# The first chunk of the projections, started on two token tiles instead of four

## The chip, the cores and the metric

One core of one Trainium2 chip runs the whole kernel in one launch. The metric is the device time of the launch in microseconds (us), given as the median of several runs. PE is the matrix engine, PEld its weight loads, DVE the vector engine, ACT the scalar engine, POOL is GpSimd, and SP is the engine that issues most DMAs.

## The reference: what is computed

A pre-norm transformer block on 2048 tokens of width 640, in float32: attention with 32 heads of width 20, then a gated feed-forward part of width 1728.

```
x = A_x
h = x + _A_ref(_layernorm(x, axis=-1), A_wqkv, A_wo)
h2 = h + _B_ref(_layernorm(h, axis=-1), B_w_gate, B_w_up, B_w_down)
```

The change lies in the very first step: the layernorm of the first 512 tokens and their products with `A_wqkv`, which give queries, keys and values.

## The kernel before

**Precision.** PE multiplies in a rounded form of float32. An operand is therefore split into a high part (a rounded copy, written by ACT) and a low part (the operand less its high part, written by DVE or POOL). A product is then three products: high by high, low by high, high by low. `w_hi` and `w_lo` hold the two parts of `wqkv`; `z_hi` and `z_lo` hold those of the normalised and transposed tokens.

**Tiles.** Tokens come in 4 chunks of 512, each of 4 tiles of 128. `wqkv` is cut into 15 blocks of 128 columns: blocks 0 to 9 hold keys (even) and queries (odd), blocks 10 to 14 hold the values. A DMA (`load_w(i)`, L541 to L549) brings two blocks at a time into one of four buffers named `raw`; a fifth load waits until a buffer is free.

**The order of work.** The schedule is written by hand: every engine executes its instructions in the order in which the program issues them. The start of the projections (L814 to L838) goes so. SP issues the loads of the four token tiles (`load_x(0)`), then four weight loads. POOL fills 32 rows twice in `k_stk` with ones (`fill_ones`, L153). PE runs three plain float32 products whose result is not used (`warm`, L820), on the token tile that is loaded last. `norm(0)` computes mean and variance of all four tiles on DVE (L137, L138), then one reciprocal square root for all four by 14 small DVE instructions (L111), then normalises the four tiles (L574). ACT writes the high parts of weight blocks 0 and 1 (L826). `flip_tokens(t)` (L624) transposes a tile on PE in five pieces (L628) into a two-bank PSUM buffer; ACT writes its `z_hi` and DVE its `z_lo` (L101, L102). After the third tile, `first_blocks` (L720) multiplies blocks 0 and 1 with the 256 tokens of the first two tiles, high by high alone. The low parts of weight blocks 0 and 1 follow on DVE (L833).

**The first slots.** The rest of the chunk is a list of 18 slots. Slot 0 issues `split_w` for blocks 2 to 5 (high parts on ACT, low parts on DVE), then the remaining `first_blocks` products for blocks 0 and 1, then `keep` for both, which takes a finished block out of PSUM, splits it, and sends it to DRAM from POOL's queue. Slot 1 frees the PSUM banks of `flip_tokens` and hands them to a pool of six single banks. Slots 2 to 9 are blocks 2 to 9 by `query_key`, then 8 slots of values. From block 6 on `split_w` puts the low parts on POOL.

**`rounds`** (L658) issues the 15 products of a block in halves: one on the upper 64 rows of the array now, the other half on the lower 64 rows 20 steps later (`LAG`), so that two halves of different products run side by side. Blocks rotate over three PSUM banks.

**The jobs in between.** In the gaps of this stream a planner places the search for score maxima that the later softmax needs (`max_four`: four products on PE, two ACT passes, four more products and two DVE reductions at L250). The planner keeps a modelled clock for each engine (`takes`). A job is placed when its keys and queries have been loaded back from DRAM, and a load may be issued from a slot that `stored_at` names. What is left of these jobs at the end runs in a closing loop; then attention begins.

Of the kernel before, what the change touches and what calls it, by code (L numbers as in the profile page):

```python
# [9 lines left out]
F32 = mybir.dt.float32  # L10
# [7 lines left out]
P = 128  # L18
S = 2048
D = 640  # L20
# [33 lines left out]
def tile_block(ctx: ExitStack, tc: tile.TileContext, x, wqkv, wo, wg, wu, wd, out):  # L54
# [27 lines left out]
    ps_ctx = ExitStack()  # L82
    flip_ctx = ExitStack()
    psum_two, psum_wide = (
        c.enter_context(tc.tile_pool(name=name, bufs=n, space=bass.MemoryType.PSUM))
        for c, name, n in ((ps_ctx, "psum_o", 2), (flip_ctx, "psum_w", 3))
    )
# [314 lines left out]
    with tc.tile_pool(name="pa", bufs=2) as pa:  # L402
# [7 lines left out]

        def load_x(c):
            for t in range(c * TPC, (c + 1) * TPC):
                xs[t] = x_tile()[:, :D]
                nc.sync.dma_start(xs[t], x[t * P : (t + 1) * P, :])
# [228 lines left out]
        LAG = 20  # L643
        given = [0, 0, 0]

# [49 lines left out]

        firsts = []

# [11 lines left out]

        def first_blocks(*hns):  # L710

            if not firsts:
                firsts.extend(ps_one() for _ in range(2))
            z_hi, z_lo = zs[0]
            for h, n in hns:
                cols = slice(h * CH // 2, (h + 1) * CH // 2)
                a, w = ((z_hi, w_hi), (z_lo, w_hi), (z_hi, w_lo))[n]
                for m, ps in enumerate(firsts):
                    for k in range(ND):
                        nc.tensor.matmul(  # L720
                            ps[:, cols], w[:, k, m * P : (m + 1) * P], a[:, k, cols],
                            start=(h == n == k == 0), stop=(h == 1 and n == 2 and k == ND - 1),
                        )

        def keep(c, m, ps):
# [87 lines left out]

        load_x(0)  # L814
        fill_ones(k_stk[0])
        for i in range(4):
            load_w(i)
        warm = ps_one()
        for _ in range(3):
            nc.tensor.matmul(warm, ident, xs[TPC - 1][:, :CH], start=True, stop=True)  # L820
        for _, _, f in norm(0):
            f()
        zs[0] = z_tiles(0)
        first_raw = raws.pop(0), raws.pop(1)
        for m, raw in enumerate(first_raw):
            nc.scalar.activation(w_hi[:, :, m * P : (m + 1) * P], raw, AF.Copy)  # L826
        for t in range(TPC):
            flip_tokens(t)
            if t == TPC - 2:
                first_blocks((0, 0))  # L830
        for m, raw in enumerate(first_raw):
            cs = slice(m * P, (m + 1) * P)
            nc.vector.tensor_tensor(  # L833
                out=w_lo[:, :, cs], in0=raw, in1=w_hi[:, :, cs].bitcast(F32), op=ALU.subtract
            )
# [4 lines left out]
        first = [("block", 0), ("none",)] + [("block", m) for m in range(2, 2 * ND)]  # L840
        some_keys = [("block", 2 * i) for i in range(ND)]
# [3 lines left out]
        for c in range(NC):  # L845
            lns = []
            work = (some_keys + some_queries if c else first) + parts
            if c == NC - 1:
# [3 lines left out]
                es.insert(1, z_tiles(NC)[0][:, :2])  # L852
            for j, (kind, *which) in enumerate(work):
                slot[0] = 18 * c + j
                while flips and not j:
                    flips.pop(0)()
                if c == 0 and j < 9:
                    for i in range(split_at[j], split_at[j + 1]):
                        split_w(i + 2)
# [18 lines left out]
                if which:  # L878
                    if (c, j) == (0, 0):
                        first_blocks((0, 1), (1, 0), (1, 1), (0, 2), (1, 2))  # L880
                        for m, ps in enumerate(firsts):
# [3 lines left out]
                else:  # L885
                    flip_ctx.close()
                    psum = ps_ctx.enter_context(
                        tc.tile_pool(name="psum", bufs=1, space=bass.MemoryType.PSUM)
                    )
                    turn, jobs, three = [0], [0], [0]  # L890

# [4 lines left out]
                    def ps_max():  # L896
                        n = turn[0] % 5
                        turn[0] += 1
                        if n > 2:
                            return psum_two.tile([P, CH], F32, name="ps_max", tag="ps_two")  # L900
                        three[0] += 1
                        return psum.tile([P, CH], F32, name="ps_max", tag=f"ps_max{three[0] % 3}")

# [51 lines left out]
    def ps_max():  # L955
        place[0] += 1
        return psum.tile([P, CH], F32, name="ps_max", tag=f"ps_max{place[0] % 3}")

# [1072 lines left out]
```

## Time and profile before

| | us |
|---|---|
| median of 3 runs | 2005.8 |
| the 3 runs | 2005.49, 2005.8, 2006.61 |
| the profiled execution, its own time | 2004.65 |
| span of its trace | 2002.9 |
| PE busy in the span | 1981.1 (99%) |
| DVE busy | 1604.4 (80%) |
| ACT busy | 1430.4 (71%) |
| POOL busy | 786.2 (39%) |

The span runs from the first to the last instruction of the trace; the execution's own time is 1.75 us longer. In a timeline row the first number is the start in us from the span's start, the second the length, then engine, line, operation, out<-in, shapes and a count when several like instructions were merged; the bracket at the end gives the idle time before and what ended it. In a row of windows each engine has its busy time with the number of instructions in brackets, followed by the clock granted to PE, the busy share of the DMA engines and GB/s. An instruction of PE or DVE shows a length that includes its way through the pipeline, so that the next one starts before its end; the distance between starts is the cost of one in a row of many.

### The profile page before, as it was taken

How to read it: one execution, taken by the hardware profiler on the slowest of the kernel's cores; microseconds unless marked ns; L12 is line 12 of the kernel's file. 1: busy time of each engine (PE TensorE's matmuls, PEld its weight loads, DVE VectorE, ACT ScalarE, POOL GpSimd, SP SyncE). 2: the span in 40 equal slices, each digit the busy share in tenths (PEclk: the TensorE clock that was granted, in tenths of full speed). 3: DMA queues.
4: the chain of work that ended last, by engine and by line, in shares of the span. 5: the costliest groups of instructions: out<-in, count | busy, mean ns of one | idle time of the engine just before them, and what ended most of it. 6: DMA issues, size and time to landing. Idle time of an engine off the chain costs nothing.

```text
span 2002.9 us, 41974 instructions
## 1 busy us (share of the span) xinstructions
PE 1981.1 (99%) x14792; PEld 1260.4 (63%) x14792; DVE 1604.4 (80%) x2873; ACT 1430.4 (71%) x2828; POOL 786.2 (39%) x1152
## 2 busy tenths in 40 slices
PE   8999999999999999999999999999999999999998
PEld 6999996444444444444444444455688888888887
DVE  5687778999999999999999999975478666677667
ACT  4677778999999999999999999977633221212221
POOL 6564423243252343334342111011255544844465
PEclk9999999999999999999999999999999999999999
DMA  7787563442533544435345222221268645974542
GB/s 239 258 258 258 176 208 90 129 121 97 161 104 114 150 135 130 130 111 157 120 134 161 79 73 60 77 67 59 65 207 291 235 159 180 358 243 166 199 147 93
DMA packets 197066, 310.50 MB, mean 155 GB/s; under 512 B 51368, under 2 KB 85480, under 8 KB 195832
## 3 DMA queue, kind: packets, MB, share of 16 engines
q1 hardware_dynamic: 190264, 284.21, 43.9%
q0 software_dynamic: 6496, 23.60, 3.9%
q8 instruction: 118, 1.93, 0.4%
q14 instruction: 92, 0.75, 0.1%
q10 hardware_dynamic: 96, 0.00, 0.0%
HBM read 208.11 MB, written 99.19 MB: 153 GB/s over the span
## 4 chain that ended last, share of the span: by engine, by line
PE 90%; DVE 1%; POOL 1%; ACT 1%; DMA 1%; issue 0%; SPq 0%; DVEq 0%; POOLq 0%; ACTq 0%
PE acc L1307 25%; PE ps_a L1494 15%; PE ps_one L1297 12%; PE ps_max L289 9%; PE ps_b L1588 8%; PE ps_max L261 7%; PE ps_one L667 7%; PE ps_max L228 3%; PE ps_max L1028 2%; PE ps_b L1028 1%; DMA t_d<-kept 0%; POOL h L1626 0%; DVE tmp L1709 0%; PE ps_max L1063 0%; POOL yp L102 0%
## 5 line engine op out<-in xcount | busy, mean ns | idle before, releaser
L1303 ACT ACTIVATE probs<-ps_one 128x512 f32<-128x512 f32 x2048 | 1049.2, 615 | 43.0 <-PE ps_one L1297 33.9
L267 DVE TENSOR_REDUCE found<-ps_max 128x1 f32<-128x512 f32 x980 | 630.4, 685 | 81.1 <-PE ps_max L261 63.7
L1297 PE MATMUL ps_one<-q_stk,k_stk 62*128 62x512 f32 x2048 | 571.9, 427 | 0.2 <-ACT probs L1303 0.2
L1307 PE MATMUL acc<-probs,v_stk 128*32 128x512 f32 x4096 | 546.6, 605 | 0.0
L289 PEld LDWEIGHTS ps_max<-k_stk,q_stk 60*128 60x128 f32 x984 | 181.8, 185 | 407.1 <-DVE found L267 402.7
L261 PE MATMUL ps_max<-k_stk,q_stk 60*128 60x512 f32 x980 | 392.9, 422 | 0.0
L298 DVE TENSOR_REDUCE found<-ps_max 128x2 f32<-128x512 f32 x492 | 335.1, 681 | 0.0
L289 PE MATMUL ps_max<-k_stk,q_stk 60*128 60x256 f32 x984 | 324.1, 329 | 0.0
L1297 PEld LDWEIGHTS ps_one<-q_stk,k_stk 62*128 62x128 f32 x2048 | 301.7, 184 | 20.0 <-ACT probs L1303 16.2
L1709 DVE TENSOR_TENSOR tmp<-ps_a,tmp 128x512 f32<-128x512 f32 x208 | 141.1, 689 | 119.7 <-PE ps_a L1494 94.0
L250 DVE TENSOR_REDUCE mx<-ps_max 128x2 f32<-128x512 f32 x288 | 180.7, 685 | 69.1 <-PE ps_max L228 61.8
L261 PEld LDWEIGHTS ps_max<-k_stk,q_stk 60*128 60x128 f32 x980 | 181.0, 185 | 52.1 <-DVE found L298 21.6
L1588 PE MATMUL ps_b<-halves,yp 128*128 128x320 f32 x1032 | 179.3, 308 | 2.0 <-POOL yp L102 1.2
L240 ACT ACTIVATE ps_max<-ps_max 128x512 f32<-128x512 f32 x288 | 151.4, 584 | 40.9 <-PE ps_max L228 38.9
L1588 PEld LDWEIGHTS ps_b<-halves,yp 128*128 128x128 f32 x1032 | 165.1, 188 | 18.7 <-POOL yp L102 1.5
L1494 PE MATMUL ps_a<-t,units 128*128 128x512 f32 x624 | 162.6, 396 | 0.0
L1307 PEld LDWEIGHTS acc<-probs,v_stk 128*32 128x32 f32 x4096 | 81.0, 108 | 128.5 <-issue 118.3
L102 POOL TENSOR_TENSOR yp<-y,yp 128x256 fp32r<-128x256 f32 x96 | 60.2, 627 | 188.2 <-ACT yp L101 188.2
L1494 PE MATMUL ps_a<-z,units 128*128 128x512 f32 x516 | 133.9, 394 | 0.0
L1494 PEld LDWEIGHTS ps_a<-t,units 128*128 128x128 f32 x624 | 112.5, 188 | 18.6
L1342 POOL TENSOR_TENSOR o<-o,rb 128x512 f32<-128x512 f32 x31 | 39.8, 1285 | 212.1 <-DMA q_stk<-q_d 80.0
L319 POOL CAST both<-neg 128x16 fp32r<-128x16 f32 x22 | 4.3, 197 | 299.0 <-DVE neg L309 243.5
(220 smaller groups left out, 3077.3 us busy)
## 6 DMA issues: line engine op xcount, KB each, us to landing
units<-w_d SPq DMA_DIRECT2D x186, 256.0 KB
w_d<-stage SPq DMA_DIRECT2D x106, 256.0 KB
halves<-j_d SPq DMA_DIRECT2D x70, 320.0 KB
j_d<-stage SPq DMA_DIRECT2D x42, 320.0 KB
k_stk<-k_d SPq DMA_DIRECT2D x64, 160.0 KB
q_stk<-q_d SPq DMA_DIRECT2D x64, 160.0 KB
raw<-k_d SPq DMA_DIRECT2D x62, 160.0 KB
raw<-q_d SPq DMA_DIRECT2D x54, 160.0 KB
```

The costliest lines, as they stand in the source:

```text
L240: nc.scalar.activation(ps, ps, AF.Relu)
L250: nc.vector.tensor_reduce(mx[:, b, :, t, kc], ps.rearrange("p (j n) -> p j n", j=2), axis=AX.X, op=ALU.max,)
L261: nc.tensor.matmul(ps, queries[u][rows, pair, t * P : (t + 1) * P], keys[u // NC][rows, pair, kc * CH : (kc + 1) * CH], start=True, stop=True,
L267: nc.vector.tensor_reduce(found_of(u)[:, b, pair, t, kc : kc + 1], ps, axis=AX.X, op=ALU.max)
L289: nc.tensor.matmul(ps[:, b * CH // 2 : (b + 1) * CH // 2], queries[u][rows, pair, t * P : (t + 1) * P], keys[u // NC][rows, pair, first : ...
L298: nc.vector.tensor_reduce(found_of(u)[:, :, pair, t, column], ps.rearrange("p (b n) -> p b n", b=2), axis=AX.X, op=ALU.max,)
L1297: nc.tensor.matmul(ps, keys[u // NC][rows, p, kt * P : (kt + 1) * P], queries[u][rows, p, :], start=True, stop=True,)
L1303: nc.scalar.activation(probs[p][:, b, :], ps, AF.Exp, scale=scale)
L1307: nc.tensor.matmul(acc[32 * j : 32 * j + 32, :], values[u // NC][:, kt, j * VW : j * VW + 32], probs[j // 2][:, j % 2, :], start=(kt == 0) ...
L1494: nc.tensor.matmul(ps.rearrange("p (t n) -> p t n", t=TPC), w[k][:, i], z[k][:, :, j], start=(first and m == 0), stop=(last and m == len(n ...
L1588: nc.tensor.matmul(ps, a, b, start=(n == 0), stop=(n == len(pairs) - 1))
L1709: add = lambda out, ps, x: nc.vector.tensor_tensor(out=out, in0=ps, in1=x, op=ALU.add)
```

## The change

1. **Loads.** SP issues token tiles 0 and 1, the first weight load (blocks 0 and 1), tiles 2 and 3, then the other three weight loads.
2. **Warming products.** Two instead of three, on token tile 1 instead of tile 3.
3. **Normalisation in two halves.** `first_tokens((0, 1))` and later `first_tokens((2, 3))` replace `norm(0)`: each has 11 small instructions and two normalisations, all of them `scalar_tensor_tensor` or `tensor_tensor` on DVE. In a normalisation the second tensor operand is the reciprocal root, broadcast to 640 columns.
4. **Four blocks by 256 tokens.** Blocks 0 to 3 are now all computed by `first_blocks`. With the first two token tiles PE does all three parts for blocks 0 and 1, and two parts for blocks 2 and 3; the rest follows in slot 0. Blocks 2 and 3 have their own two PSUM banks (`psum_pair`); `flip_tokens` keeps two buffers instead of three.
5. **Low parts.** POOL writes those of blocks 0 and 1, then 2, 3, 6 and 7; before each of the two groups POOL copies one column of a normalised token tile (`behind_tile`), which makes it wait for that normalisation. DVE writes blocks 4 and 5. High parts of blocks 2 to 7 are issued on ACT ahead of tiles 2 and 3.
6. **Planner.** Slots 2 and 3 are empty and cost nothing; the modelled PE clock is charged 3510 and 4680 ns for slot 0. `stored_at` names slot 5 instead of 4 for group 0, the one group of four heads that lies wholly in blocks 0 and 1; the other groups keep their slots.
7. **PSUM pools.** The six single banks become four on the left and two (`ps_max1`, `ps_max2`) on the right, where `psum_pair` was.

```diff
-                return 2 * block + 4 + (block > 0)
+                return 2 * block + 5
...
-        given = [0, 0, 0]
+        given = [0]
...
+        def first_tokens(ts, mv):
+
+            n = len(ts)
+            v, r, t = (pa.tile([P, n], F32, name=f"{x}_first", bufs=2) for x in "vrt")
+            var = mv[:, ts[0] : ts[-1] + 1, 1]
+            stt = nc.vector.scalar_tensor_tensor
+            stt(v, var, EPS, var, op0=ALU.add, op1=ALU.max)
+            stt(r.bitcast(I32), v.bitcast(I32), -0.5, magic[:, :n], op0=ALU.mult, op1=ALU.add)
+            for _ in range(3):
+                nc.vector.tensor_tensor(out=t, in0=r, in1=r, op=ALU.mult)
+                stt(t, t, -0.5, v, op0=ALU.mult, op1=ALU.mult)
+                stt(r, t, 1.5, r, op0=ALU.add, op1=ALU.mult)
+            for i, k in enumerate(ts):
+                stt(
+                    xs[k], xs[k], mv[:, k, 0:1], r[:, i : i + 1].to_broadcast([P, D]),
+                    op0=ALU.subtract, op1=ALU.mult,
+                )
...
-        load_x(0)
+        load_x(0, 0, 2)
+        load_w(0)
+        load_x(0, 2, TPC)
+        for i in range(1, 4):
+            load_w(i)
         fill_ones(k_stk[0])
-        for i in range(4):
-            load_w(i)
         warm = ps_one()
-        for _ in range(3):
-            nc.tensor.matmul(warm, ident, xs[TPC - 1][:, :CH], start=True, stop=True)
+        for _ in range(2):
+            nc.tensor.matmul(warm, ident, xs[1][:, :CH], start=True, stop=True)
...
+        def behind_tile(t):
+            nc.gpsimd.tensor_copy(pa.tile([P, 1], F32, name="seen", bufs=1), xs[t][:, :1])
...
+        first_stats(0)
+        first_stats(1)
+        first_tokens((0, 1), moments)
+        first_high(0, 1)
+        behind_tile(1)
+        first_low(nc.gpsimd, 0, 1)
+        first_stats(2)
+        flip_tokens(0)
+        flip_tokens(1)
+        first_stats(3)
+        first_tokens((2, 3), moments)
+        for m in (2, 4, 6):
+            first_high(m, m + 1)
+        behind_tile(3)
+        first_low(nc.gpsimd, 2, 3, 6, 7)
+        first_blocks((0, 1), (0, 0), (0, 1), (0, 2))
+        first_blocks((2, 3), (0, 0))
+        first_blocks((2,), (0, 1))
+        flip_tokens(2)
+        first_blocks((3,), (0, 1))
+        flip_tokens(3)
+        first_low(nc.vector, 4, 5)
...
-                        first_blocks((0, 1), (1, 0), (1, 1), (0, 2), (1, 2))
-                        for m, ps in enumerate(firsts):
-                            keep(0, m, ps)
+                        for ms in ((0, 1), (2, 3)):
+                            first_blocks(ms, (1, 0), (1, 1))
+                            if ms[0]:
+                                first_blocks(ms, (0, 2))
+                            first_blocks(ms, (1, 2))
+                            takes("PE", 3510 + 1170 * (ms[0] > 0))
+                            for m in ms:
+                                keep(0, m, firsts[m])
```

In `first_blocks(ms, (h, n), ...)` the pair names the half of the 512 tokens (h) and the part (n: 0 high by high, 1 low tokens by high weights, 2 high tokens by low weights).

More of the change, by code (lines that the diff above doesn't have):

```diff
@@ L694, in query_key @@
             )
-        firsts = []
+        firsts = {}
         def split_later(f, ready):
@@ L708, in finish_splits, with first_blocks @@
                 splits.pop(0)[1]()
-        def first_blocks(*hns):
-            if not firsts:
-                firsts.extend(ps_one() for _ in range(2))
+        def first_blocks(ms, *hns):
             z_hi, z_lo = zs[0]
@@ L823, in tile_block @@
         zs[0] = z_tiles(0)
[L824 to L835, printed above, removed]
+        magic = pa.tile([P, 2], F32, name="magic", bufs=1)
@@ new lines, in tile_block, with first_high, first_low @@
+        nc.vector.memset(magic, 1597463007.0)
+        first_raw = {}
+        def first_high(*ms):
+            for m in ms:
+                first_raw[m] = raws.pop(m)
+                nc.scalar.activation(w_hi[:, :, m * P : (m + 1) * P], first_raw[m], AF.Copy)
+        def first_low(engine, *ms):
+            for m in ms:
+                cs = slice(m * P, (m + 1) * P)
+                engine.tensor_tensor(
+                    out=w_lo[:, :, cs], in0=first_raw[m], in1=w_hi[:, :, cs].bitcast(F32),
+                    op=ALU.subtract,
+                )
@@ new lines, in behind_tile, with first_stats @@
+        def behind_tile(t):
+            nc.gpsimd.tensor_copy(pa.tile([P, 1], F32, name="seen", bufs=1), xs[t][:, :1])
+        moments = pa.tile([P, TPC, 2], F32, name="mv")
+        def first_stats(t):
+            stats(pa, xs[t], moments[:, t, :])
+        for m in range(2):
+            firsts[m] = ps_one()
+        pair = psum_pair.tile([P, 2, CH], F32, name="ps_pair")
+        for m in range(2):
+            firsts[2 + m] = pair[:, m]
+        first_stats(0)
+        first_stats(1)
+        first_tokens((0, 1), moments)
@@ L839, in tile_block @@
         parts = [("value", *divmod(i, 2)) for i in range(2 * TPC)]
-        first = [("block", 0), ("none",)] + [("block", m) for m in range(2, 2 * ND)]
+        first = [("block", 0), ("none",), (), ()] + [("block", m) for m in range(4, 2 * ND)]
         some_keys = [("block", 2 * i) for i in range(ND)]
@@ L852, in tile_block @@
                 es.insert(1, z_tiles(NC)[0][:, :2])
-            for j, (kind, *which) in enumerate(work):
+            for j, (kind, *which) in enumerate(w or ("empty",) for w in work):
                 slot[0] = 18 * c + j
@@ L901, in ps_max @@
                         three[0] += 1
-                        return psum.tile([P, CH], F32, name="ps_max", tag=f"ps_max{three[0] % 3}")
+                        return max_bank(three[0])
                 if c == 0 and j == 6:
@@ L956, in ps_max @@
         place[0] += 1
-        return psum.tile([P, CH], F32, name="ps_max", tag=f"ps_max{place[0] % 3}")
+        return max_bank(place[0])
     pp = att_ctx.enter_context(tc.tile_pool(name="pp", bufs=6, side="right"))
```

37 lines of the change are left out of this document (23 added, 14 removed).

## The prediction

> **What bounds the kernel now.** I read the page first, then the front of the trace in windows and in order of time.
>
> ```profile
> span 2002.9 us, 41974 instructions
> PE 1981.1 (99%) x14792; PEld 1260.4 (63%) x14792; DVE 1604.4 (80%) x2873; ACT 1430.4 (71%) x2828; POOL 786.2 (39%) x1152
> PE 90%; DVE 1%; POOL 1%; ACT 1%; DMA 1%; issue 0%; SPq 0%; DVEq 0%; POOLq 0%; ACTq 0%
> ```
>
> PE sets the end: 99% busy, and 90% of the chain. Its work is the same after the change, but for one warming product, so the change is worth the PE time that it frees at the front, less what comes back later.
>
> ```profile
> 0.00:5.00 5.00, 0.00 (x0) 0.00 (x0) 1.42 (x5) 1.28 (x1) 4.29 (x8) 1.00 0.62 180
> 5.00:10.00 5.00, 2.51 (x3) 1.17 (x4) 4.04 (x17) 0.75 (x2) 3.42 (x1) 1.00 1.02 345
> 10.00:15.00 5.00, 4.70 (x20) 2.57 (x18) 4.00 (x12) 1.99 (x4) 0.00 (x0) 1.00 0.82 261
> 15.00:20.00 5.00, 5.00 (x43) 5.00 (x44) 3.90 (x7) 3.52 (x6) 0.00 (x0) 1.00 0.00 0
> ```
>
> The first number behind the comma is PE: nothing in 5 us, then warming products, and useful work only from the third row. The same stretch in order of time:
>
> ```profile
> 0.76 1.82 SPq L414 DMA_DIRECT2D xt<-in_A_x  x4
> 1.38 7.05 POOL L153 MEMSET k_stk<- 32x4096 f32 x2
> 3.61 0.89 DVE L137 BATCH_NORM_STATS2 st<-xt 128x6 f32<-128x320 f32 x2 [2.73 <-DMA xt<-in_A_x]
> ...
> 4.66 0.83 DVE L137 BATCH_NORM_STATS2 st<-xt 128x6 f32<-128x320 f32 x2
> 5.52 0.21 DVE L138 BATCH_NORM_AGGREGATE mv<-st 128x2 f32<-128x12 f32 x1
> 6.31 0.89 DVE L137 BATCH_NORM_STATS2 st<-xt 128x6 f32<-128x320 f32 x2 [0.58 <-DMA xt<-in_A_x]
> ...
> 7.49 5.46 PE L820 MATMUL ps_two<-xt,ident 128*128 128x512 f32 x6 [7.49 <-DMA xt<-in_A_x]
> ...
> 8.54 0.17 DVE L111 TENSOR_SCALAR v_a<-mv 128x4 f32<-128x4 f32 x1
> ...
> 9.25 1.36 ACT L826 ACTIVATE w_hi<-raw 128x640 fp32r<-128x640 f32 x2 [7.22 <-DMA raw<-in_A_wqkv]
> ...
> 11.34 2.26 DVE L574 TENSOR_SCALAR xt<-xt,mv,r_a 128x640 f32<-128x640 f32 x4
> ...
> 12.74 1.94 PE L628 MATMUL ps_wide<-ident,xt 128*128 128x128 f32 x15
> ...
> 13.62 1.90 ACT L101 ACTIVATE z_hi<-ps_wide 128x640 fp32r<-128x640 f32 x3 [3.01 <-PE ps_wide L628]
> 14.36 2.29 DVE L102 TENSOR_TENSOR z_lo<-ps_wide,z_hi 128x640 fp32r<-128x640 f32 x3 [0.76 <-ACT z_hi L101]
> ...
> 14.98 1.44 PE L720 MATMUL ps_two<-z_hi,w_hi 128*128 128x256 f32 x10 [0.30 <-ACT z_hi L101]
> ...
> 17.99 1.34 PE L720 MATMUL ps_two<-z_hi,w_hi 128*128 128x256 f32 x10
> ...
> 19.16 1.34 PE L720 MATMUL ps_two<-z_lo,w_hi 128*128 128x256 f32 x10
> ...
> 22.79 1.43 PE L667 MATMUL ps_one<-z_hi,w_hi 64*128 64x512 f32 x5
> ...
> 29.89 0.39 PE L667 MATMUL ps_one<-z_hi,w_hi 64*128 64x512 f32 x1
> ```
>
> DVE waits for four tiles (to 8.5), computes the roots (2.8 us), and only then does PE get its first transpose, at 12.74. From there PE hardly stops. Ten products of 256 columns cost 17.99 to 19.16 = 1.17 us: I call this a unit. Block 2 starts at 22.79, and 30 half products of blocks 2 and 3 later block 4 starts at **29.89**. What follows block 4 is the same PE work in both kernels, and so is the lag of 20 halves, which is paid once. So I compare the start of block 4.
>
> **The change, step by step.** *DVE to the first normalised tile.* Tile 1 is there by 4.66; its statistics end at 5.52 + 0.21 = 5.7. The 14 small instructions took 8.54 to 11.34, 0.2 each; 11 take 2.2, to 7.95. The normalisation as a `scalar_tensor_tensor` is not in the trace. It lies between 0.57 (2.26/4, one operand, L574) and the 0.76 of the two-operand subtraction (2.29/3); I take 0.75, since it too reads two tensors: tiles ready at 8.7 and 9.5.
>
> *PE's warming products* start with tile 1 at 4.66; six rows took 12.74 - 7.49 = 5.25, so four take 3.5, to 8.2. They end before the tile is ready.
>
> *Transposes and first product.* Five pieces cost 0.11 each (1.94/15, less the tail of the last), ACT's copy followed the first transpose by 0.88, and one copy costs 0.6 to 0.7. So with transposes from 8.95, `z_hi` of both tiles is there at 11.15, and the first product at 11.2. Weights: the first block takes tile 2's place in the queue; with 1.8 us a load (it was there 9.25 - 7.49 after tile 3) it comes at 7 to 8, and ACT's two high parts (1.36) end by 9.4, ahead of 11.2. Tiles 2 and 3 move behind it by as much: to 8.1 and 9.3. DVE reaches them at 9.5 and 12.1.
>
> *DVE's second half:* statistics of tile 2 to 10.5, `z_lo` of tiles 0 and 1 to 12.1, statistics of tile 3 to 13.1, 11 small ones to 15.3, two normalisations to 16.1 and 16.9.
>
> ```profile
> 13.50:14.00 0.50, 0.50 (x7) 0.50 (x6) 0.10 (x1) 0.38 (x1) 0.00 (x0) 1.00 0.51 160
> 14.00:14.50 0.50, 0.50 (x7) 0.44 (x5) 0.14 (x1) 0.50 (x2) 0.00 (x0) 1.00 0.08 25
> 27.95 9.19 POOL L102 TENSOR_TENSOR w_lo<-raw,w_hi 128x640 fp32r<-128x640 f32 x6
> 20.10 11.33 SPq L547 DMA_DIRECT2D raw<-in_A_wqkv  x4
> ```
>
> The fourth weight load has left the queue by about 14.3 (DMA share 0.51, then 0.08), as it will after the change. A low part costs POOL 9.19/6 = 1.53.
>
> *PE's queue.* High by high for blocks 0 and 1 to 12.4; low by high (`z_lo` at 12.1) to 13.6; high by low to 14.7 (POOL's low parts start behind tile 1 at 9.6 and end at 12.9: covered by 0.7 us); one and a half units for blocks 2 and 3 to 16.5; transposes of tile 2 (ready 16.1) to 17.1; half a unit to 17.7; tile 3 to 18.2. ACT's high parts of blocks 2 to 7, of which the last two wait for that fourth load, end about 16.2, before tile 2's copy is wanted at 17.3. `z_hi` of tile 3 at 19.2: PE stands for 1.0. Then three units for blocks 0 and 1 and four for blocks 2 and 3: 19.2 + 8.2 = 27.4. POOL's second group waits for tile 3 at 16.9 and has blocks 2 and 3 by 20.2, five us before PE asks. Behind it POOL has blocks 6 and 7, then the stores of `keep`; DVE's low parts of blocks 4 and 5 are wanted only at 29.7. The nearest cover is 0.7 us, so I add 0.3 for handoffs between engines: **27.7 against 29.89, a gain of 2.2 us**.
>
> *Queues passed.* `fill_ones` keeps its place on POOL. SP's fifth weight load went out at 20.10, when DVE gave back the first buffer; POOL gives it back at 12.9, so all later loads come earlier and nobody waits for them longer.
>
> The profiled execution took 2004.65 (1.75 beyond the span), so it would take 2002.45; the median lies 1.15 higher, hence **2003.6**. About 0.2%, 4.0 us, is what a measurement of this kernel can tell from no change; the forecast lies inside.
>
> **Clock.** The sum takes PE at the speed of the rows from 13 us on. Before that it was slower:
>
> ```profile
> 12.74:13.00 0.26, 0.26 (x2) 0.26 (x2) 1.00 1.11 351
> 13.00:13.26 0.26, 0.26 (x4) 0.26 (x3) 1.00 1.09 347
> L820 PEld LDWEIGHTS ps_two<-xt,ident x6: 288/333/338, 7.5 to 11.0; 128*128 128x128 f32 x6
> L628 PEld LDWEIGHTS ps_wide<-ident,xt x20: 140/141/226, 12.0 to 16.6; 128*128 128x128 f32 x20
> ```
>
> Half as many transposes fall into the quarter microsecond before 13.0 as into that after, and the same weight load took 333 ns during the warming products and 141 later. The clock column shows 1.00 throughout, but PE became twice as fast at 13.0, 5.5 us after its first product. Now the warming lasts 3.5 us, and PE has gaps before and after the transposes. [...]
>
> **Rivals.** *1. PE is still slow when the products begin.* For: the 5.5 us just read. Against: the 5.25 us were one uninterrupted run, of which 3.5 may have been enough. Price: the transposes take 0.22 each, so the first product starts 0.95 later, at 12.1; if the count begins anew there, PE becomes fast 3.5 to 5.5 us later and loses half of that, 1.75 to 2.75. The start of block 4 moves to 30.4 to 31.4, 0.5 to 1.5 slower than before: 2006.3 to 2007.3, say 2006.8. It decides from a release later than 14.6 on (0.95 plus half of 2.5 us is the gain of 2.2).
>
> *2. The small instructions wait for POOL's fill.*
>
> ```profile
> 45.90 0.70 DVE L111 TENSOR_SCALAR v_a<-mv 128x4 f32<-128x4 f32 x1
> 45.85 0.72 POOL L102 TENSOR_TENSOR v_stk<-v_stk 128x256 fp32r<-128x256 f32 x1
> ```
>
> The instruction that took 0.17 at 8.54 took 0.70 here, and ended as POOL's did. Before, DVE's small ones began just after the fill's end at 8.43; now they would begin at 5.7, inside it. Held to 8.43, everything moves by 2.7: block 4 at 30.4, 2006.3. [...]
>
> *3. The maxima run late.*
>
> ```profile
> 50.08 1.29 DVE L250 TENSOR_REDUCE mx<-ps_max 128x2 f32<-128x512 f32 x2 [1.60 <-PE ps_max L228]
> 319.93 0.40 PE L228 MATMUL ps_max<-raw 60*128 60x256 f32 x2
> 320.63 1.33 PE L667 MATMUL ps_one<-z_hi,w_lo 64*128 64x512 f32 x5
> ```
>
> Group 0's load moves one slot back, 15 half products of 0.233 or 3.5 us against the projection's own stream. The last product for maxima ends at 320.3, the last projection product at 322.0: 1.7 us of slack. If no later wait for data absorbs the delay, 3.5 - 1.7 = 1.8 us comes back: 2005.4.
>
> *4. More than forecast.* With a fast clock from the first transpose and no gap at all, PE's 12 units and 20 transposes (16.2 us) from 8.95 would start block 4 at 25.2, a gain of 4.7: 2001.1. It needs `z_hi` without delay, which ACT's 0.7 per tile speaks against.
>
> **How the numbers follow.** Forecast 0.45, rival 1 0.27, rival 2 0.05, rival 3 0.13, rival 4 0.07, and 0.03 for a planner's order that costs over 4 us. The range 2001.6 to 2007.4 takes in rivals 1 to 3 with their bounds and half the way to rival 4. Slower than before by any amount: 0.35. Over 4 us faster: rival 4 and the lower edge of the forecast, 0.10; over 4 us slower: 0.04; within: 0.86.
>
> **What would show it.** Right: first transpose near 9, first L720-like product near 11.2, one PE gap of about 1 us near 18 to 19, block 4 near 27.7, and the last projection product near 319.8. Rival 1: transposes 0.22 apart from 9 on, and ten products taking 2.3 at first. Rival 2: the first small DVE instruction ends at 8.4. Rival 3: reductions of L250 after the last projection product. A wait of PE for POOL's low parts, or a normalisation above 0.8 us, would break the sum.

## The result, and the profile after

| | before | after |
|---|---|---|
| median, us (lowest to highest of 4 runs) | 2005.64 (2003.98 to 2006.61) | **2026.81** (2025.1 to 2029.55) |
| ratio | | 1.0108, 95% interval 1.009 to 1.0125 |
| the profiled execution, its own time | 2004.65 | 2026.44 |
| span of its trace | 2002.9 | 2024.6 |

The changed kernel is 21 us slower. The forecast was 2003.6, its range 2001.6 to 2007.4. The page of the changed kernel, the three lines that the prediction began with:

```profile
span 2024.6 us, 41992 instructions
PE 1988.0 (98%) x14790; PEld 1266.7 (63%) x14790; DVE 1611.0 (80%) x2878; ACT 1431.9 (71%) x2828; POOL 793.6 (39%) x1158
PE 85%; DMA 1%; POOL 1%; DVE 1%; issue 1%; ACT 1%; SPq 0%; POOLq 0%; DVEq 0%; ACTq 0%
```

PE issues two matmul records less and is busy 6.9 us longer (1988.0 against 1981.1); its idle time in the span grew from 21.8 to 36.6, by 14.8. Both together are the 21.7 us of the span. So PE did the same work, waited more, and did part of it more slowly.

**The front.** The start of the changed kernel, in order of time:

```profile
6.31 0.16 DVE L732 SCALAR_TENSOR_TENSOR v_first<-mv 128x2 f32<-128x2 f32 x1
...
8.47 1.68 DVE L739 SCALAR_TENSOR_TENSOR xt<-xt,mv,r_first 128x640 f32<-128x640 f32 x2
...
9.41 1.67 PE L631 MATMUL ps_wide<-ident,xt 128*128 128x128 f32 x10 [0.58 <-DVE xt L739]
...
11.92 1.46 PE L721 MATMUL ps_two<-z_hi,w_hi 128*128 128x256 f32 x10 [0.84 <-ACT z_hi L104]
...
28.42 1.43 PE L670 MATMUL ps_one<-z_hi,w_hi 64*128 64x512 f32 x5
```

The first product comes 3.06 us earlier (11.92 against 14.98) and block 4 starts at 28.42 against 29.89: 1.47 us gained. The front did what it was to do. The loss lies behind it.

**Two places where PE stands.** The windows of the changed kernel (PE's busy time is the first number behind the comma, the granted clock the third from the end), then what PE waited for in 55 to 75 us and in 318 to 345 us. A wait's three numbers are its sum, how often it came and the longest:

```profile
60.00:65.00 5.00, 3.47 (x45) 3.18 (x45) 2.51 (x4) 2.39 (x5) 4.39 (x6) 1.00 0.83 243
65.00:70.00 5.00, 0.96 (x6) 0.46 (x6) 3.75 (x4) 0.00 (x0) 0.98 (x3) 0.82 0.89 301
70.00:75.00 5.00, 4.95 (x44) 4.95 (x46) 0.00 (x0) 2.59 (x5) 3.30 (x4) 0.50 0.73 261
...
330.00:335.00 5.00, 2.53 (x15) 1.75 (x13) 3.16 (x7) 2.45 (x5) 4.36 (x6) 0.95 0.56 144
335.00:340.00 5.00, 0.55 (x2) 0.53 (x4) 0.00 (x0) 0.00 (x0) 4.95 (x2) 0.50 0.50 140
340.00:345.00 5.00, 4.98 (x23) 2.17 (x19) 3.87 (x6) 4.03 (x8) 1.51 (x1) 0.53 0.25 70
```
```profile
PE ps_max L606 <- DVE xt L577: 5.6, 4, 3.7
...
PE ps_one L1371 <- DMA q_stk<-m: 5.5, 1, 5.5
PE ps_max L292 <- DVE m L105: 1.4, 1, 1.4
```

Two of these windows in the kernel before:

```profile
65.00:70.00 5.00, 4.04 (x52) 3.66 (x51) 1.99 (x4) 3.68 (x8) 2.91 (x5) 1.00 0.88 335
330.00:335.00 5.00, 5.00 (x41) 1.87 (x40) 4.63 (x9) 4.95 (x11) 1.79 (x1) 1.00 0.00 1
```

The kernel before has a full clock in all six windows, and its longest wait there is 1.0 us. In the changed kernel a wait of 5.6 us in four parts is followed by 5 us in which PE is busy and its clock stands at 0.50 (half clock from here on); a wait of 5.5 us is followed by the same. At half clock two half products of 320 columns, side by side, start every 0.27 us (72.09 to 72.36), at the full clock every 0.15 (75.89 to 76.04). So each of these two stalls cost its own length, and then again a part of the work that fell into the slow stretch. That part is counted as half of the work in what follows, which is an estimate; by the two figures it is 0.12 of 0.27.

*Stall one, 63 to 75 us.* PE wants to transpose the second chunk's token tiles (L606), and DVE has not normalised them (L577). The queues of GpSimd and DVE, first in the kernel before, then in the changed one:

```profile
56.50 0.20 POOL L111 TENSOR_TENSOR r_a<-r_a,t_a 128x4 f32<-128x4 f32 x1
...
57.87 3.86 DVE L574 TENSOR_SCALAR xt<-xt,mv,r_a 128x640 f32<-128x640 f32 x4
58.92 1.85 POOL L102 TENSOR_TENSOR e<-e 128x768 fp32r<-128x768 f32 x1 [0.18 <-ACT e L101]
```
```profile
59.30 0.20 POOL L114 TENSOR_TENSOR t_a<-t_a,v_a 128x4 f32<-128x4 f32 x1
59.45 1.82 POOL L105 TENSOR_TENSOR e<-e 128x768 fp32r<-128x768 f32 x1
61.56 1.24 POOL L642 DMA_DIRECT2D k_d<-e  x2 [0.29 <-POOL e L105]
62.81 1.28 POOL L105 TENSOR_TENSOR v_stk<-v_stk 128x512 fp32r<-128x512 f32 x1
64.39 1.19 POOL L642 DMA_DIRECT2D q_d<-v_stk  x2 [0.29 <-POOL v_stk L105]
65.61 0.20 POOL L114 TENSOR_SCALAR t_a<-t_a 128x4 f32<-128x4 f32 x1
65.90 0.20 POOL L114 TENSOR_TENSOR r_a<-r_a,t_a 128x4 f32<-128x4 f32 x1
66.13 3.86 DVE L577 TENSOR_SCALAR xt<-xt,mv,r_a 128x640 f32<-128x640 f32 x4 [1.51 <-POOL r_a L114]
```

The planner put the last two of the small root steps (the instructions of the reciprocal square root, 0.2 us each) behind two splits and four stores of `keep`. Those take from 59.45 to 65.6. Before, all root steps were through at 56.7, ahead of them.

*Stall two, 331 to 345 us.* The end of the projections in the changed kernel:

```profile
331.08 0.62 PE L670 MATMUL ps_one<-z_hi,w_lo 64*128 64x512 f32 x2
331.37 0.57 PE L231 MATMUL ps_max<-raw 60*128 60x256 f32 x3
331.87 0.28 PE L348 MATMUL ps_max<-ident,neg 128*16 128x128 f32 x1
...
335.24 2.94 SPq L355 DMA_DIRECT2D q_stk<-m  x4
...
339.45 0.76 PE L1371 MATMUL ps_one<-q_stk,k_stk 62*128 62x512 f32 x1 [5.49 <-DMA q_stk<-m]
```

`max_finish(0)` (the transpose at L348, then four DMAs of the maxima into `q_stk`, which the first attention product reads) comes behind the last projection product. Before, it stood at 316.1, 5.5 us ahead of that product, and attention began at once at 321.92:

```profile
316.10 0.28 PE L345 MATMUL ps_max<-ident,neg 128*16 128x128 f32 x1
...
321.92 0.50 PE L1297 MATMUL ps_one<-q_stk,k_stk 62*128 62x512 f32 x1
```

The cause is one line of the planner, `finish_at = min(finish_at, slot[0] + 2)`. The chunks have slots 0 to 71. Before, group 0's last job fell into slot 69, so the finish into 71. Now it falls into slot 70, and 72 does not exist, so the finish waits for the end of the closing loop.

The sum by the trace: block 4 starts 1.47 us earlier, the last projection product 9.8 later (331.32 against 321.56), the first attention product 17.5 later, PE's last product 21.8 later. So 11.2 us went in the projections, 7.8 at stall two, and 4.3 in what follows. Of the 11.2, the waits of stall one are 5.6, half of the 5.6 us that PE worked at half clock behind it (68.2 to 75.0) is 2.8, and 1.9 is a wait for ACT between 108 and 122; the rest, 0.9, is not assigned. Of the 4.3, half the time that PE worked at half clock (339.45 to 344.7) is 2.6.

### The profile page after: what moved, and what is told of

Same layout as the page of the kernel before. It is cut to its first block, busy times and chain, and to the rows that moved or that the text cites. A ratio compares the mean times of both kernels' runs of the same rounds, so it can differ in the third digit from the quotient of the medians.

```text
span 2024.6 us, 41992 instructions
## 1 busy us (share of the span) xinstructions
PE 1988.0 (98%) x14790; PEld 1266.7 (63%) x14790; DVE 1611.0 (80%) x2878; ACT 1431.9 (71%) x2828; POOL 793.6 (39%) x1158
## 4 chain that ended last, share of the span: by engine, by line
PE 85%; DMA 1%; POOL 1%; DVE 1%; issue 1%; ACT 1%; SPq 0%; POOLq 0%; DVEq 0%; ACTq 0%
PE acc L1381 25%; PE ps_a L1568 15%; PE ps_one L1371 12%; PE ps_max L292 9%; PE ps_b L1662 8%; PE ps_max L264 7%; PE ps_one L670 4%; PE ps_max L1102 2%; PE ps_max L231 1%; PE ps_b L1102 1%; DMA halves<-j_d 1%; DMA o_t<-o_d 0%; POOL h L1700 0%; SPq L1327 0%; PE ps_max L1137 0%
```

## The experiments

The kernel before ran beside each group on the same chip: 2005.19 us with `a_norm`, `a_slot`, `a_both` and `b_late`; 2004.71 with `a_fin`, `b_fin`, `a_dve` and `a_nf`; 2005.06 with `a_root`, `b_root`, `a_rootfin` and `a_tune2`; 2005.05 with `a_warm` and `b_both`. Each ratio below is against the kernel before in the same group. Names with `a_` are edits of the changed kernel, names with `b_` of the kernel before.

### Undoing the two edits of the plan

The due date is the time of the modelled PE clock from which the planner may place the steps of the second chunk's normalisation. It is set at the start of slot 3, 15 us of modelled time ahead. Before, slots 2 and 3 cost the modelled clock 3475 ns each (6950 in all), so that block 4 began 3475 ns behind that point; now slots 0 to 3 cost 8190 ns, all of it in slot 0, and block 4 begins at that point. So the due date, measured from block 4, came 3475 ns later. `a_norm` moves it back by as much. `a_slot` gives group 0's load its slot 4 back. `a_both` does both.

```diff
-                    x_there[0] = clock["PE"] + X_LANDING
+                    x_there[0] = clock["PE"] + X_LANDING - (0 if c else 3475)
...
-                return 2 * block + 5
+                return 2 * block + 4 + (block > 0)
```

> The changed kernel, with the modelled time at which the steps of the second chunk's normalisation come due moved 3475 ns earlier, so that it lies as far ahead of block 4 as it did before the change; nothing else. Theory A (the hand-written plan charges slot 0 with all four blocks and so places the last reciprocal-root steps on GpSimd behind two more stores; PE then waits for the normalised tokens for 5.6 us and runs at half clock for 6.8 us after that): the wait of PE for the normalised tokens near 63 to 70 us falls below 1 us, the half clock near 68 us is gone, the time falls by 8 to 10 us to 2017 to 2019; the 5.5 us wait before attention stays. Rival B (GpSimd itself is late since it now writes more low parts, whatever the plan says): a wait of over 3 us stays there and the time stays above 2022.

> The changed kernel, with group 0's keys and queries loaded from slot 4 again instead of slot 5; nothing else. Theory A: the first products for maxima come about one block earlier (32 half products), the wait for the normalised tokens stays at 4 to 6 us, and since the transposition of the first maxima still stands behind the closing loop, the wait before attention stays: 2024 to 2028. Rival C (the slot alone delayed the maxima and so made both waits): both waits shrink and the time falls below 2015.

> Both edits of the two kernels before in one. In the order of its instructions the transposition of the first maxima stands 20 half products ahead of the end of the projections again, and the last root steps stand ahead of two stores. Theory A: neither wait is left, PE never falls to half clock between 15 us and the end, and what is left is the gain of the front, 1.5 us: 2003 to 2006. Rival B: a wait of over 3 us near 63 us stays, above 2010.

| | median, us | ratio to before, interval |
|---|---|---|
| `a_norm` | 2020.83 | 1.0082, 1.0067 to 1.0097 |
| `a_slot` | 2021.9 | 1.0082, 1.0067 to 1.0097 |
| `a_both` | 2010.75 | 1.0028, 1.0017 to 1.0039 |

One edit alone brings 6.0 and 4.9 us, both together 16.1. They do not add up: with either edit alone a part of stall one stays (2.6 us of waits ahead of the second chunk's transposes in `a_norm`, 3.5 in `a_slot`), and group 0's last job still falls into slot 70; with both it falls into slot 69. In `a_both` neither stall is left (`max_finish` stands at 318.4, and this is all of the wait ahead of the transposes):

```profile
PE ps_max L606 <- DVE xt L577: 0.9, 1, 0.9
```

None of the three came out as forecast in time. `a_norm` lost the half clock near 68, but its wait stayed over the 1 us that was expected, and its time over 2017 to 2019. `a_slot` was faster than 2024 to 2028. `a_both` was expected at 2003 to 2006 and is still 5.6 us slower than the kernel before, so the two plan edits are not the whole loss. By its trace it started block 4 1.6 us earlier than the kernel before, lost 3.9 us from there to the last projection product, and 3.8 after the start of attention, where its clock fell to half from 327.5 to 334.4.

### The later due date in the kernel before

`b_late` adds 3475 ns to the due date in the kernel before.

> The kernel before the change, with the steps of the second chunk's normalisation due 3475 ns later in the modelled clock, which is what the changed kernel's plan amounts to; all else as before. PE's order is the same as before. Theory A: PE waits 3 to 6 us for the normalised tokens near 64 us and loses up to 3.4 us more at half clock: 2009 to 2015. Rival B: no such wait, 2005 to 2007.

2005.06 us, ratio 0.9998 (0.9988 to 1.0008), where 2009 to 2015 was expected. The theory that the due date alone makes stall one fell: here the wait ahead of the transposes is 1.05 us. All root steps still precede the splits and stores on GpSimd's queue. What counts is which instruction ends up in front of which, and a later date changes that only in some plans.

### Both plan edits in the kernel before

`b_both` has the kernel before's front, the due date of `b_late` and group 0's load in slot 5.

> The kernel before with the change's two edits of the plan alone: due date of the second chunk's normalisation 3475 ns later, group 0's load in slot 5. The front is untouched. Its order on GpSimd has all root steps ahead of the splits and stores, and max_finish(0) behind the closing loop. If the end of the plan is what these edits cost by themselves: wait of 5.5 us ahead of attention, under 2.5 us of waits for the second chunk's transposes, 2005 + 9.5 = 2012 to 2017. If they cost what the change cost: over 2022. If they cost nothing without the changed front: under 2008.

2020.84 us, ratio 1.0077 (1.0062 to 1.0093): more than the end of the plan alone would cost. What its PE waited for, in 55 to 75 and in 318 to 345 us:

```profile
PE ps_max L603 <- DVE xt L574: 2.5, 2, 1.9
...
PE ps_one L1297 <- DMA q_stk<-m: 5.5, 1, 5.5
```

With an untouched front, 15.8 of the 21 us are there, with half clock for 6.8 us from 66.8 on and for 10.2 us from 333.0 on. Three quarters of the loss come from the two plan edits alone. Stall one has another order behind it here: all root steps stand ahead of the splits on GpSimd (the last one ends at 58.6), but on DVE the last two normalisations stand behind four reductions and start at 65.8.

### Stall two by itself

`a_fin` keeps `max_finish(0)` in slot 71 in the changed kernel; `b_fin` pushes it out of the last slot in the kernel before. `a_nf` is `a_fin` with the due date of `a_norm`.

```diff
-                    finish_at = min(finish_at, slot[0] + 2)
+                    finish_at = min(finish_at, slot[0] + 2, 18 * NC - 1)
```

and in `b_fin`

```diff
-                    finish_at = min(finish_at, slot[0] + 2)
+                    finish_at = min(finish_at, slot[0] + 3)
```

> The changed kernel with one edit: max_finish(0) is placed in slot 71 at the latest, the last one, instead of falling behind the closing loop (the planner reached the last job of group 0 in slot 70 instead of 69, and 70 + 2 is a slot that does not exist). Theory B (the wait ahead of attention is the way of the maxima through DVE and DMA, laid bare because max_finish stands last): PE's waits of 5.5 and 1.4 us ahead of the first attention product shrink to under 2, no half clock behind them, first attention product at 331 to 333 instead of 339.4, time 2013 to 2017. Rival (the maxima themselves are late, their place in the program is not the matter): the wait stays over 4 us, time over 2022. The stall at 63 to 75 us stays as it is under both (about 5.6 us of waits and half clock).

> The kernel before with one edit: max_finish(0) is pushed one slot further, which puts it behind the closing loop as in the changed kernel; nothing else moves. Theory B: PE waits 5 to 7.5 us ahead of attention (DMA of the maxima into q_stk), and the granted clock then falls to half for 7 to 10 us: 2005.2 + 7 + 4 to 5 = 2015 to 2018, slower by 0.5 to 0.65%. Rival (attention absorbs the wait, since the work behind it is the same and other products can go ahead): under 2009. If the wait comes without half clock: 2011 to 2013.

> The changed kernel with two edits: the due date of the second chunk's normalisation moved back to where it stood (3475 ns earlier), and max_finish(0) in slot 71 at the latest; group 0's load stays one slot later. If the two stalls are separate and add up: 2026 - 6 (measured for the due date alone) - 10 to 13 = 2007 to 2010. If they are one and the same delay (each edit alone gives what both give): 2013 or more.

`b_fin`: 2014.16 us, ratio 1.0042 (1.0028 to 1.0056), 9.5 us from moving one step. Its waits and the windows behind them:

```profile
PE ps_one L1297 <- DMA q_stk<-m: 5.5, 1, 5.5
PE ps_max L289 <- DVE m L102: 1.7, 1, 1.7
```
```profile
318.00:323.00 5.00, 3.09 (x15) 1.99 (x13) 2.25 (x6) 1.87 (x4) 4.04 (x5) 1.00 0.60 152
323.00:328.00 5.00, 0.00 (x0) 0.00 (x0) 0.23 (x1) 0.00 (x0) 4.89 (x3) 0.50 0.52 139
328.00:333.00 5.00, 4.74 (x19) 2.70 (x23) 3.51 (x6) 3.91 (x8) 2.31 (x1) 0.50 0.32 98
333.00:338.00 5.00, 5.00 (x31) 2.31 (x24) 2.43 (x5) 2.43 (x6) 0.00 (x0) 0.64 0.01 3
```

This is stall two of the changed kernel, in a kernel that is otherwise the one before. From the last projection product to PE's last product it takes 11.3 us longer than the kernel before: the waits are 7.2, and half of the 8.4 us that PE worked at half clock is 4.2. The median is just under the forecast of 2015 to 2018. `a_fin`: 2022.73 us, ratio 1.0086 (1.0071 to 1.0101): the wait of 5.5 is gone, as theory B has it, but only 4.1 us came back where 10 to 14 were expected, and the time is in the range of the rival. A wait of 1.3 us for DVE stayed, which had the reductions of the last jobs in front, with 6.8 us of half clock behind it, and in this execution PE waited 2.1 us more at 59 for a late load. `a_nf`: 2017.55, ratio 1.0061 (1.0046 to 1.0076), where 2007 to 2010 was expected. The two stalls are separate, since both edits bring 9.3 us where each alone brings 6.0 and 4.1; but they are not all, since `a_both` is 6.8 us faster than `a_nf`.

### Stall one: low parts, or the order in the queues?

`a_dve` takes the low parts of blocks 2, 3, 6 and 7, and the wait for tile 3, off GpSimd. `a_root` lets the planner place four normalisation steps per slot in the first chunk, `b_root` two in the kernel before (with `max_finish` kept in slot 71). `a_rootfin` is `a_root` with the edit of `a_fin`.

```diff
-        behind_tile(3)
-        first_low(nc.gpsimd, 2, 3, 6, 7)
...
-        first_low(nc.vector, 4, 5)
+        first_low(nc.vector, 2, 3, 4, 5, 6, 7)
```
```diff
-                    steps_due[0] = 3
+                    steps_due[0] = 3 if c else 4
```

> The changed kernel with GpSimd relieved: the low parts of blocks 2, 3, 6 and 7 go to DVE behind those of tile 3, and the wait of GpSimd for tile 3 is gone; GpSimd keeps blocks 0 and 1. The plan is untouched. Theory P (the stall ahead of the second chunk's transposes needs GpSimd to be late): GpSimd's root steps come at least 3 us earlier than 56.6 to 66.1, the waits at 63 to 70 (5.6 us) shrink to under 3, no half clock at 68, time 2019 to 2022; the wait ahead of attention stays. Theory A (the plan's later due date alone sets it): waits over 5 us, time 2025 or more. Block 4 of the first chunk starts at 28.4 or up to 1 us earlier under both.

> The changed kernel with one number altered: the planner may place four steps of the second chunk's normalisation per slot instead of three (first chunk only). Due dates, loads and the front stay; on GpSimd's queue the last two root steps now stand ahead of the split of 768 columns, the split of v_stk and the four stores that held them in the changed kernel from 59.3 to 65.6. Theory R (it is this order on GpSimd's queue that makes the stall, neither the low parts nor the due date as such): last root step by 60.5, PE's waits at 63 to 70 fall from 5.6 to under 2, no half clock at 68, time 2018 to 2020.5. Rival (the normalisation is late on DVE as well): waits over 4, time over 2023. The wait ahead of attention stays in both.

> The kernel before with the opposite: two normalisation steps per slot in the first chunk instead of three, which puts the last two root steps behind the same splits and stores on GpSimd's queue; max_finish(0) is kept in slot 71. The front is untouched. Theory R: PE waits 4 to 6 us ahead of the second chunk's transposes, half clock of 3.4 to 6.8 us behind it, 2005 + 6 to 9 = 2011 to 2014. Rival (the stall needs the changed front): waits under 2, time under 2007.

> The changed kernel with four steps per slot and max_finish(0) in slot 71 at the latest: both stalls taken away where they arise, while due date and load slot stay as the change has them. If the two account for the loss: 2026.8 - 7.5 - 4.5 (the latter measured for max_finish alone) = 2013 to 2016. If the later due date and load slot cost something of their own, it shows as what is left over 2013.

`a_dve`: 2026.58 us, ratio 1.0107 (1.0092 to 1.0122), no change. That GpSimd is late because of the low parts that the change gave it was my own theory, and it fell. Its last root step:

```profile
65.67 0.20 POOL L114 TENSOR_TENSOR r_a<-r_a,t_a 128x4 f32<-128x4 f32 x1
```

It ends 0.2 us earlier than in the changed kernel: the order in front of it is the same. `b_root`: 2013.94 us, ratio 1.0049 (1.0035 to 1.0062), within the 2011 to 2014 of theory R. The old front with the last two root steps behind the same splits and stores has the stall, and 3.4 us of half clock from 68.2 on:

```profile
PE ps_max L603 <- DVE xt L574: 4.4, 4, 2.4
```

Not all of its 8.9 us belong to stall one: PE also waited 2.0 us for DVE ahead of attention, with 3.4 us of half clock behind it (331.1 to 334.5), and 1.3 us for late loads near 178.

`a_root`: 2022.01 us, ratio 1.0087 (1.0073 to 1.0101); 4.8 us came back, the wait fell from 5.6 to 4.0 only, where under 2 was expected, and 6.8 us of half clock from 67.9 on stayed. DVE's queue shows why:

```profile
58.97 0.20 POOL L114 TENSOR_TENSOR r_a<-r_a,t_a 128x4 f32<-128x4 f32 x1
```
```profile
62.66 1.29 DVE L253 TENSOR_REDUCE mx<-ps_max 128x2 f32<-128x512 f32 x2 [4.31 <-PE ps_max L231]
64.68 1.29 DVE L253 TENSOR_REDUCE mx<-ps_max 128x2 f32<-128x512 f32 x2 [0.73 <-PE ps_max L231]
65.89 3.85 DVE L577 TENSOR_SCALAR xt<-xt,mv,r_a 128x640 f32<-128x640 f32 x4
```

GpSimd is through at 59.2, but DVE stands 4.31 us before a reduction, waiting for PE, with the four normalisations behind it. In the kernel before they stand ahead of the reductions (57.87). So the order in two queues makes the stall: `b_root` shows it for GpSimd's, and `a_root` and `b_both` for DVE's. `a_rootfin`: 2017.71, ratio 1.0071 (1.0058 to 1.0085), above the expected 2013 to 2016. What it is above 2013, 4.7 us, is not settled piece by piece; a wait of 4.2 us for the normalisations is left, and one of 2.7 for a late load at 59.7, where the changed kernel had none.

### A repaired plan, and the front's clock

`a_tune2` has group 0's load in slot 4, the due date 1500 ns earlier, and the splits of blocks 8 and 9, with a weight load behind them, issued between the `keep`s of blocks 0, 1 and of 2, 3 (and the limit of `a_fin`, which changes nothing there). `a_warm` is `a_tune2` with 22 warming products of `ident` by `ident` instead of two on token tile 1.

```diff
...
+                            if ms[0] == 0:
+                                split_w(8)
+                                split_w(9)
+                                load_w(loaded)
+                                loaded += 1
...
```
```diff
-        for _ in range(2):
-            nc.tensor.matmul(warm, ident, xs[1][:, :CH], start=True, stop=True)
+        for _ in range(22):
+            nc.tensor.matmul(warm[:, :P], ident, ident, start=True, stop=True)
```

> The changed kernel, its plan repaired and more: group 0's load in slot 4 again, the due date 1500 ns earlier, and the low parts of blocks 8 and 9 ahead of the stores of blocks 2 and 3 on GpSimd's queue, so that weight buffers come free earlier for the loads of group 0. With due date and load slot alone repaired it was 2010.75, of which about 3.9 us were lost between the start of block 4 and the last projection product (waits for late loads at 46 and 51, for ACT at 108). Theory: the late loads are GpSimd's order, so the waits at 46 and 51 go: 2007 to 2009.5; if PE also gets through the start of attention without half clock, 2004 to 2006, level with before. Rival (these waits have another cause): 2010 to 2012.

> The kernel with the repaired plan (due date 1500 ns earlier, group 0's load in slot 4, low parts of blocks 8 and 9 ahead of the stores) and other warming products: 22 small ones of ident by ident, which need no load and can start at 1.4 us instead of two on token tile 1 from 4.8 us on. In the repaired kernel's profiled execution the clock was full from 8.3, half from 11.7 to 15.1, and block 4 started at 29.62; in the changed kernel's it was full from 10.2 on and block 4 started at 28.42. Theory C (what is left over the kernel before, 2.2 us, is the front's clock, which the two short warming products hold only in some executions): full clock from 9 us or earlier without a half stretch behind it, block 4 at 28.5 or earlier, median 2005 to 2006.5, level with the kernel before. Rival (the rest lies elsewhere, in the start of attention): block 4 earlier, but median 2007 or more.

`a_tune2`: 2007.29 us, ratio 1.0014 (1.0005 to 1.0023). The waits for late loads are gone, and the last projection product stands at 321.4, 9.9 us earlier than in the changed kernel. Why loads were late, the first load of group 0's keys shows, in the kernel before, then in the changed kernel, there with GpSimd's low parts of weights:

```profile
34.11 1.86 SPq L164 DMA_DIRECT2D raw<-k_d  x4
```
```profile
39.74 1.47 SPq L167 DMA_DIRECT2D raw<-k_d  x4
36.62 7.67 POOL L105 TENSOR_TENSOR w_lo<-raw,w_hi 128x640 fp32r<-128x640 f32 x5
```

The slot moved this load by only 1.0 us (in `a_both` it goes out at 38.77). The buffer that it needs is given back by low parts on GpSimd, which began at 27.95 before; in the changed kernel they begin at 36.62, behind the stores of blocks 2 and 3, and the second of them is through when the load goes out. In `a_tune2` the load goes out at 35.73. But in this execution the clock, full from 8.3 on, fell back at 11.7:

```profile
12.00:15.00 3.00, 3.00 (x16) 3.00 (x16) 2.65 (x13) 2.38 (x4) 1.25 (x1) 0.50 0.74 222
```

Block 4 started at 29.62, and the front's gain was gone. In the nine other profiled executions with these two warming products the clock stayed full there. Nor does this trace put all that is left over the kernel before at the front, as theory C has it: the first attention product comes at 321.79, level with 321.92 before, and 2.6 us are lost behind it, with half clock from 325.7 to 329.2. `a_warm`: 2005.73 us, ratio 1.0002 (0.9993 to 1.0011):

```profile
1.37 7.67 PE L841 MATMUL ps_two<-ident 128*128 128x128 f32 x44 [1.37 <-POOL ident masks.py:199]
9.00 1.56 PE L631 MATMUL ps_wide<-ident,xt 128*128 128x128 f32 x10
...
27.86 1.43 PE L670 MATMUL ps_one<-z_hi,w_hi 64*128 64x512 f32 x5
```

Warming that needs no load runs up to the transposes, the clock was full from 6.6 to 324.1, and block 4 started at 27.86, 2.0 us earlier than before. The median is level with the kernel before. The last projection product is 1.1 us earlier, the first attention product 0.5; in this execution 3.4 us of half clock at the start of attention (324.1 to 327.5) take more than that, and PE's last product comes 1.5 us later than before. So the median fits theory C, but the trace puts what is left at the start of attention, as its rival does. Whether the gain is lost there in most executions stays open, and so do the 1.7 us that the changed kernel loses after the start of attention beyond its half clock.

## Why the prediction was wrong, point by point

- **The step that failed:** "What follows block 4 is the same PE work in both kernels ... So I compare the start of block 4." The work was the same; its order was not. The change touched the planner's clock, a due date that is reckoned from it, and a load slot, and everything behind block 4 is placed by these. The two edits of the plan cost 15.8 us in the kernel before (`b_both`) and give back 16.1 when undone (`a_both`). Beyond them `a_both` still lies 5.6 us over the kernel before: it spends the front's gain and more on short waits in the projections (the longest 1.7 us, for ACT at 108) and behind the start of attention.
- **The sum at the front** held in its mechanism. First transposes at 9.41 where about 9 was forecast, first product at 11.92 for 11.2, PE's gap at 19.2 of 0.79 for 1.0, block 4 at 28.42 for 27.7. The mis-sized terms: token tile 0 came 0.5 us later, a normalisation took 0.84 (1.68 for two) for 0.75, over the 0.8 that the prediction named as breaking its sum, at a price of 0.2.
- **"... all later loads come earlier and nobody waits for them longer"** failed too. It followed the weight loads alone. The first load of group 0's keys went out 5.6 us later (39.74 against 34.11), since low parts of later blocks stood behind more stores on GpSimd's queue. In `a_both` PE waited 0.9 us for such loads near 46 and 0.8 us for DVE at 51; in `a_tune2` it waited for neither.
- **Rival 1** (half clock at the first products) did not come in this execution, where the clock was full from 10.2 on, but did in that of `a_tune2`, where it was at half from 11.7 to 15.1. In the nine other profiled executions with two such products the clock stayed full there. That 3.5 us of warming may be enough was the author's estimate, and no run shows by what the clock is set: the first of the two products started at 5.07 and the clock was full 5.1 us later (10.2); in `a_tune2` it started at 4.83 and the clock was full 3.5 us later (8.3), but fell back at 11.7.
- **Rival 2** fell: the small DVE instructions ran at 0.16 us each while GpSimd's fill ran to 8.43. Its chance of 0.05 was the author's estimate.
- **Rival 3** (group 0's load a slot later) had the right place and a wrong price. It gave 1.8 us for a delay in which the maxima shift by as much as the load does. But the plan works in steps: two root steps slipped behind 6 us of GpSimd work, and the finish slipped past the last slot.
- **The chance of 0.03 for "a planner's order that costs over 4 us"** was the case that happened. It was given no mechanism. The rows for one stood in the profile: the root steps end at 56.7, the next split on that queue starts at 58.92, and `max_finish` ran 5.5 us ahead of the last product. Each row says how little the plan may slip.
- **Half clock** was counted for the front alone, and not behind PE's later waits.

## What to carry to other kernels

When a schedule is placed by a modelled clock, an edit that changes a cost, a due date or a slot is an edit to the order of everything behind it. Compare that order instruction by instruction, in every engine's queue, before counting the gain as lasting. Look for rules with a cliff, such as "two slots later", and for small instructions that a matrix engine will wait for, and see what stands in front of them. Look also at the clock behind a stall of PE: in `b_fin` the waits of 7.2 us and half of the 8.4 us of PE work at half clock behind them, 4.2, make 11.4, and the trace lost 11.3.

## What the runs showed of the hardware that was not expected

The half clock came in pieces of about 3.4 us: 6.8 from 68.2 on and 10.2 from 334.5 on in the changed kernel, 13.7 from 323.0 on in `b_fin`, 3.4 from 11.7 on in `a_tune2`. From the first full clock at 10.2 to the fall at 68.2 are 58.0 us, 17 such pieces. The wait of 5.5 us in the changed kernel cost about half as much again in slow products: 5.2 us of PE's work after 339.45 were done at half clock, of which half is 2.6. Not every fall had a long wait ahead of it: in `a_root` the clock fell at 61.0 for 3.4 us, when PE had not waited over 0.7 us at a time. At the start of attention the clock fell for 3.4 us in `a_warm` and `a_tune2` and for 6.8 us in `a_both`, with no wait of PE over 0.6 us ahead of it, and did not fall in the kernel before; what tells these executions apart was not found.
